# Selective attention and feed-forward on one core: from a planned order to a hand-ordered pipeline of heads and feed-forward pieces

## The chip, the cores and the metric

The kernel runs on one core of one Trainium2 chip. A core has engines that run side by side, each in the order of its own queue: TensorE (PE in the profile; PEld are its weight loads) multiplies matrices and transposes, VectorE (DVE) and ScalarE (ACT) work element by element and read PSUM, where PE writes its results, GpSimd (POOL) works element by element in SBUF, and SyncE (SP) issues the transfers between HBM and SBUF. An engine waits for another through semaphores. The metric is the device time of one execution in microseconds; the time given is the median of several executions.

## What is computed

For 8 batches of 8 heads, with 576 tokens and a head size of 64, causal attention gets a bias from cumulative sums of a positive score `s`. The heads, side by side, are the 512 features of a token. A normalised copy goes through a feed-forward of 2,048 hidden features, and the features themselves are added.

```python
scores = scale * np.matmul(q, k.transpose(0, 1, 3, 2))
s_pos = np.maximum(s, 0.0)
cum = np.cumsum(s_pos, axis=-1)
bias = -(cum[:, :, :, None] - cum[:, :, None, :])
scores = np.where(causal, -1000000000.0, scores + np.minimum(bias, 0.0))
scores = scores - np.max(scores, axis=-1, keepdims=True)
attn = np.exp(scores)
attn = attn / (np.sum(attn, axis=-1, keepdims=True) + 1e-09)
x = np.matmul(attn, v)            # heads laid side by side: (8, 576, 512)
...
xn = (x - mu) / np.sqrt(var + 1e-06) * g_ln
out = x + np.maximum(xn @ w_ch1, 0.0) @ w_ch2
```

Inputs and output are f32; the kernel multiplies in bf16.

## The kernel before

A sequence of 576 tokens is cut in tiles of 128: four full ones and one of 64 (`tsz`). The program is written as one straight sequence, and a scheduler of the framework orders the instructions of each engine from the data dependences and the number of buffers of each pool. So neighbouring heads, and the end of one batch and the start of the next, may be mixed in a queue.

**Preparation.** The first weight is loaded in four pieces of 1 MB, scaled by `g_ln` on VectorE (line 75) and cast on ScalarE (78); the second comes in 16 pieces of 256 KB with casts on ScalarE (84). The cumulative sums of all 64 heads are made at once, in ten doubling steps (94, 95), and put into HBM, once in f32 and once, negated, in bf16.

**Attention**, for each batch: 15 tiles of q, k and v are loaded by SyncE through three buffers and cast on ScalarE (135 to 145). For each head, ten PE transposes (159), each with a copy out of PSUM by VectorE or ScalarE (164), make `qT` and `kT`, 64 rows of 576 columns. A 65th row holds the negated sums in `qT`, brought by a small transfer (152), and ones in `kT`, a memset on GpSimd (151). Five small transfers bring the sums of the keys as a column (172). For each of five key blocks, PE makes the transposed scores for this and all later queries (185), 1,600 columns a head in six matmuls; ScalarE takes the exponential with the keys' sums as bias (194), and GpSimd zeroes what lies above the diagonal (201). Then 15 matmuls of 65 columns multiply by v, whose 65th column of ones gives the denominator (218), and VectorE divides, tile by tile (226, 227).

**Normalisation**, for each batch and tile: statistics on VectorE (238, 240), a square root on ScalarE (242), the normalised row in bf16 (251), four transposes (261) with a copy each (266).

**Feed-forward**, for each batch: 16 blocks of the hidden features, each with four matmuls of 512 columns and four of the 64 left over (277), and a relu of 576 columns on ScalarE (285). Then, for each of five tiles, 16 matmuls of 512 columns (291), the sum with `x_acc` on VectorE (299) and the transfer out (300). The last tile has 64 tokens, and its 16 matmuls still have 512 columns.

## Time and profile before

| what | value |
|---|---|
| median of three executions | 765.15 us (764.25 to 766.16) |
| span of the profiled execution | 764.1 us, 11,760 instructions |
| GpSimd busy | 124.0 us |
| transfers by SP's queue | 46.76 MB in 163,520 packets, 26.6% of 16 engines' span |
| HBM | 37.07 MB read, 9.66 MB written |
| line 277, all forms | 1,000 matmul records, 150.8 us busy |
| line 218, all forms | 960 matmul records, 133.7 us busy |

The profile comes from one further execution, and its span is set beside the median. An engine's busy time is the sum of its instructions' durations; matmuls are pipelined, so that PE may be busy and yet not at its peak, and a matmul's duration holds a delay that the next one overlaps. The pitch, from one start to the next, is then the better measure. The granted clock is the share of TensorE's full clock that it was given.

A row of the grouped instructions reads: line, engine, operation, result <- operands, form, count | busy us, mean ns of one | idle us of the engine just before, and what ended it. A row of stages reads: from:to and length in us, then busy us and count for PE, PEld, DVE, ACT and POOL, then the granted clock, the busy share of the transfer engines and GB/s. A row of the timeline reads: start, length, engine, line, instruction.

### The profile page before, as it was taken

The page shows a single profiled execution, that of the slowest core. Times are in us where ns is not written, and L with a number is a line of the kernel's source. Part 1 is how long each engine was busy: PE and PEld are TensorE (multiplying, and loading weights), DVE is VectorE, ACT ScalarE, POOL GpSimd, SP SyncE. Part 2 cuts the span into 40 slices and gives each one's busy share as a digit, 9 for nine tenths or more (in the row PEclk, how much of TensorE's full clock was granted, in tenths as well). Part 3 has the DMA queues.
Part 4 walks back from the last instruction along what each step waited for, and adds up shares of the span by engine and source line. Part 5 has one row for each costly group of instructions (what it writes and reads, how often), then busy time and mean ns, then how long its engine had stood idle before and what let it go on. Part 6 is the DMA issues. An engine that isn't in the chain of part 4 may idle for free.

```text
span 764.1 us, 11760 instructions
## 1 busy us (share of the span) xinstructions
PE 653.0 (85%) x3772; PEld 323.6 (42%) x3808; DVE 290.2 (38%) x1313; ACT 422.8 (55%) x1006; POOL 124.0 (16%) x390
## 2 busy tenths in 40 slices
PE   0039989997999979998899979999799989999797
PEld 0014434443445434454344434454344544454343
DVE  5215531456015550255314560155503552145601
ACT  4656674667646576256734577065662655255650
POOL 1003300232003310033002320033100330023100
PEclk9999999755895559955697558965599557965599
DMA  9860243522471044101531034200421000100001
GB/s 310 201 134 3 43 111 74 120 43 50 79 185 28 3 84 104 62 2 16 110 91 35 2 57 113 74 9 2 94 60 54 2 2 1 42 23 1 1 1 63
DMA packets 163581, 47.51 MB, mean 62 GB/s; under 512 B 156096, under 2 KB 156224, under 8 KB 163008
## 3 DMA queue, kind: packets, MB, share of 16 engines
q1 hardware_dynamic: 163520, 46.76, 26.6%
q8 instruction: 30, 0.49, 0.3%
q14 instruction: 31, 0.25, 0.1%
HBM read 37.07 MB, written 9.66 MB: 61 GB/s over the span
## 4 chain that ended last, share of the span: by engine, by line
PE 73%; DVE 8%; ACT 7%; DMA 5%; issue 4%; POOL 2%; SPq 1%; DVEq 0%; ACTq 0%
PE ph L277 18%; PE py L291 18%; PE ps L185 13%; PE pt L159 13%; PE pot L218 9%; PE ptx L261 3%; ACT e L194 2%; DVE qT L164 2%; ACT xnT L266 2%; DVE stats L238 2%; DMA qkvtmp<-in_k_dram 2%; POOL kT L151 1%; DMA w2tmp<-in_moe_w_ch_dram 1%; DMA cum_a<-in_s_dram 1%; ACT qT L164 1%
## 5 line engine op out<-in xcount | busy, mean ns | idle before, releaser
L194 ACT ACTIVATE e<-ps,cumk 128x576 bf16<-128x576 f32 (+4 forms) x320 | 158.9, 524 | 70.2 <-PE ps L185 40.8
L201 POOL TENSOR_SCALAR_AFFINE_SELECT e<-e 128x128 bf16<-128x128 bf16 (+1 forms) x320 | 86.8, 280 | 563.0 <-ACT e L194 535.8
L277 PE MATMUL ph<-xnT,w_bf 128*128 128x64 bf16 (+1 forms) x1000 | 150.8, 306 | 1.5 <-ACT hT L285 0.6
L185 PE MATMUL ps<-qT,kT 65*128 65x512 bf16 (+5 forms) x384 | 138.6, 397 | 4.0 <-ACT e L194 3.6
L291 PE MATMUL py<-w_bf,hT 128*128 128x512 bf16 (+1 forms) x628 | 139.4, 379 | 1.0
L218 PE MATMUL pot<-v_bf,e 128*128 128x65 bf16 (+2 forms) x960 | 133.7, 247 | 7.6 <-DVE x_acc L227 3.3
L159 PE MATMUL pt<-ident,q_bf 128*64 128x128 bf16 (+1 forms) x320 | 88.6, 277 | 48.5 <-ACT q_bf L140 30.3
L299 DVE TENSOR_TENSOR yo<-py,x_acc 128x512 f32<-128x512 f32 (+1 forms) x40 | 27.6, 690 | 227.6 <-PE py L291 216.5
L218 PEld LDWEIGHTS <-e 128*128 128x128 bf16 (+2 forms) x960 | 80.2, 127 | 72.4 <-POOL e L201 20.1
L159 PE MATMUL pt<-ident,k_bf 128*64 128x128 bf16 (+1 forms) x320 | 91.1, 285 | 19.6 <-ACT k_bf L145 19.1
L277 PEld LDWEIGHTS <-w_bf 128*128 128x128 bf16 x1024 | 71.0, 103 | 72.8 <-issue 20.2
L285 ACT ACTIVATE hT<-ph 128x576 bf16<-128x576 f32 x128 | 82.9, 649 | 32.3 <-PE ph L277 32.3
L291 PEld LDWEIGHTS <-hT 128*128 128x128 bf16 (+1 forms) x640 | 62.9, 100 | 73.8 <-issue 3.4
L164 DVE COPY qT<-pt 64x128 bf16<-64x128 bf16 (+1 forms) x222 | 46.8, 211 | 112.7 <-PE pt L159 106.2
L227 DVE TENSOR_SCALAR x_acc<-pot,rinv 128x64 f32<-128x64 f32 (+1 forms) x320 | 87.8, 274 | 3.5
L226 DVE RECIPROCAL rinv<-pot 128x1 f32<-128x1 f32 (+1 forms) x320 | 53.1, 166 | 88.3 <-PE pot L218 62.8
L164 ACT COPY qT<-pt 64x128 bf16<-64x128 bf16 (+1 forms) x98 | 22.3, 228 | 93.8 <-PE pt L159 90.7
L159 PEld LDWEIGHTS <-q_bf 128*64 128x64 bf16 (+1 forms) x320 | 41.0, 130 | 65.6 <-ACT q_bf L140 31.1
L159 PEld LDWEIGHTS <-k_bf 128*64 128x64 bf16 (+1 forms) x320 | 41.8, 130 | 63.5 <-issue 34.0
L164 ACT COPY kT<-pt 64x128 bf16<-64x128 bf16 (+1 forms) x132 | 31.5, 239 | 47.9 <-PE pt L159 46.0
L261 PE MATMUL ptx<-ident,xn_bf 128*128 128x128 bf16 (+1 forms) x160 | 36.2, 266 | 25.1 <-DVE xn_bf L251 11.7
L185 PEld LDWEIGHTS <-kT 65*128 65x128 bf16 (+1 forms) x384 | 39.0, 117 | 39.3 <-issue 25.5
(33 smaller groups left out, 323.2 us busy)
## 6 DMA issues: line engine op xcount, KB each, us to landing
qkvtmp<-in_q_dram SPq DMA_DIRECT2D x32, 256.0 KB
qkvtmp<-in_k_dram SPq DMA_DIRECT2D x32, 256.0 KB
qkvtmp<-in_v_dram SPq DMA_DIRECT2D x32, 256.0 KB
out_dram<-yo SPq DMA_DIRECT2D x32, 256.0 KB
w1tmp<-in_moe_w_ch_dram SPq DMA_DIRECT2D x4, 1024.0 KB
w2tmp<-in_moe_w_ch_dram SPq DMA_DIRECT2D x16, 256.0 KB
cumk<-cum_dram SPq DMA_DIRECT2D x256, 0.5 KB
qkvtmp<-in_q_dram SPq DMA_DIRECT2D x8, 128.0 KB
```

The costliest lines, as they stand in the source:

```text
L159: nc.tensor.transpose(pt[:D, :pn], src[:pn, p, h, :], ident[:pn, :pn],)
L164: nc.any.tensor_copy(out=dst[:D, p * P : p * P + pn], in_=pt[:D, :pn])
L185: nc.tensor.matmul(ps[:kbn, o : o + w], lhsT=kT[:D1, kb * P : kb * P + kbn], rhs=qT[:D1, kb * P + o : kb * P + o + w], start=True, stop=True,)
L194: nc.scalar.activation(out=e[:kbn, :qspan], in_=ps[:kbn, :qspan], func=ACT.Exp, bias=cumk[:kbn, kb : kb + 1], scale=1.0,)
L201: nc.gpsimd.affine_select(out=e[:kbn, :kbn], in_=e[:kbn, :kbn], compare_op=ALU.is_ge, fill=0.0, base=0, pattern=[[1, kbn]], channel_multip ...
L218: nc.tensor.matmul(pot[:qn, :], lhsT=e[:kbn, off : off + qn], rhs=v_bf[:kbn, kb, h, :], start=(kb == 0), stop=(kb == t),)
L226: nc.vector.reciprocal(out=rinv[:qn], in_=pot[:qn, D : D + 1])
L227: nc.vector.tensor_scalar_mul(out=x_acc[:qn, t, h * D : (h + 1) * D], in0=pot[:qn, :D], scalar1=rinv[:qn],)
L261: nc.tensor.transpose(pt[:, :qn], xn_bf[:qn, kd * P : (kd + 1) * P], ident[:qn, :qn],)
L277: nc.tensor.matmul(ph[:, o : o + w], lhsT=w1_bf[:, kd, fb * P : (fb + 1) * P], rhs=xnT[:, kd, o : o + w], start=(kd == 0), stop=(kd == KD ...
L285: nc.scalar.activation(out=hT[:, fb, :], in_=ph, func=ACT.Relu)
L291: nc.tensor.matmul(py[:qn, :], lhsT=hT[:, fb, t * P : t * P + qn], rhs=w2_bf[:, fb, :], start=(fb == 0), stop=(fb == FB - 1),)
```

## The change

All of the kernel's body is written anew. The framework's scheduler is switched off (`manual_schedule`): each engine runs its instructions in the order in which the program names them.

- **Slots.** The main loop runs over 64 slots, one head each. A slot names: the weight pieces (batch 0 only), the casts of the tiles loaded in the slot before, two loads for the next batch, in every second slot the transposes of the next two heads, the scores of this head, two feed-forward units, the values of the head before, and two more units.
- **Units.** The feed-forward of a batch is cut in 32 units of four matmuls of 512 columns: 16 for the first layer, with the relu on VectorE in every fourth and on ScalarE otherwise, and 16 quarters of the second. The units of a batch are queued at the end of the second slot of the next one, after its normalisation (`ln_tile`), which is written tile after tile. Its statistics are made in two parts before that, the power -1/2 on GpSimd one slot earlier.
- **Chunks of 512 tokens.** A chunk is a batch's four full tiles. The last 64 tokens of two batches share a tile, `xm`, and the four such tiles are a ninth chunk, run at the end.
- **Bias as contraction rows.** `qT` and `kT` have 68 rows: `qT` holds the negated sums in bf16 and three rows of ones, `kT` ones and the keys' sums in three bf16 parts. A bias on the exponential is no longer needed, so one instruction takes 512 columns of two key blocks at a time. The rows come from SBUF by four transfers for four heads (`aug`). The sums are made by one scan.
- **Transposes for two heads**: a full 128x128 block at a time, five into one PSUM tile, and two copies of 64x640.
- **Casts** of q, k and v stand on ScalarE, VectorE and GpSimd in turn for batch 0, which comes in 30 halves ahead of the slots, and on GpSimd after it. The second weight's casts are on GpSimd too, and the first weight is scaled and cast by one VectorE instruction.

The old lines are those printed above; of the new ones, the core:

```diff
+    stage = ctx.enter_context(tc.tile_pool(name="stage", bufs=8))
+    wst = ctx.enter_context(tc.tile_pool(name="wst", bufs=2))
...
+    xtp = ctx.enter_context(tc.tile_pool(name="xtp", bufs=2))
...
+    ps_s = ctx.enter_context(tc.tile_pool(name="ps_s", bufs=3, space=bass.MemoryType.PSUM))
+    ps_m = ctx.enter_context(tc.tile_pool(name="ps_m", bufs=2, space=bass.MemoryType.PSUM))
+    ps_t = ctx.enter_context(tc.tile_pool(name="ps_t", bufs=2, space=bass.MemoryType.PSUM))
+    ps_o = ctx.enter_context(tc.tile_pool(name="ps_o", bufs=1, space=bass.MemoryType.PSUM))
+    ctx.enter_context(tc.manual_schedule())
...
+    qT = [const.tile([P, G, SP], BF16, name=f"qT{i}") for i in range(2)]
+    kT = [const.tile([P, G, SP], BF16, name=f"kT{i}") for i in range(2)]
+    e2 = [const.tile([P, 2, EW], BF16, name=f"e2_{i}") for i in range(3)]
+    xm = [const.tile([P, Dm], F32, name=f"xm{i}") for i in range(4)]
+    xTm = const.tile([P, KD, 512], BF16, name="xTm")
...
+    def load(src, b, t, h0, h1, eng):
+        pn = P if t < NF else TL
+        tmp = stage.tile([P, h1 - h0, D], F32, name="qkvtmp", tag="st")
+        eng.dma_start(
+            out=tmp[:pn],
+            in_=src[b, h0:h1, t * P : t * P + pn, :].rearrange("h s d -> s h d"),
+        )
+        return tmp, pn
+    def cast(kind, b, t, h0, h1, tmp, pn, eng):
+        if kind == "v":
+            dst = v_bf[b % 2][:pn, t, h0:h1, 0:D]
+        else:
+            dst = (q_bf if kind == "q" else k_bf)[b % 2][:pn, t, h0:h1, :]
...
+    for i in range(2):
+        nc.gpsimd.memset(q_bf[i][TL:P, NF, :, :], 0.0)
+        nc.gpsimd.memset(k_bf[i][TL:P, NF, :, :], 0.0)
+        nc.vector.memset(v_bf[i][:, 0:NF, :, D : D + 1], 1.0)
+        nc.vector.memset(v_bf[i][TL:P, NF, :, :], 0.0)
+        nc.vector.memset(v_bf[i][0:TL, NF, :, D : D + 1], 1.0)
+        nc.gpsimd.memset(qT[i][D:KA, :, :], 1.0)
+        nc.gpsimd.memset(kT[i][D:KA, :, :], 1.0)
+    for i in range(3):
+        nc.gpsimd.memset(e2[i][TL:P, :, OD : OD + TL], 0.0)
+        nc.gpsimd.memset(e2[i][:, :, OD + TL : EW], 0.0)
+    nc.vector.tensor_tensor_scan(
+        out=c_sc, data0=c_one, data1=c_in, initial=0.0, op0=ALU.mult, op1=ALU.add
+    )
...
+    def aug(b, g):
+        r0 = b * H + g * G
+        i = (b * 2 + g) % 2
+        for j, src in ((1, c_hi), (2, c_mid), (3, c_lo)):
+            nc.sync.dma_start(out=kT[i][D + j : D + j + 1, :, 0:S], in_=src[r0 : r0 + G, :])
+        nc.sync.dma_start(out=qT[i][D : D + 1, :, 0:S], in_=c_neg[r0 : r0 + G, :])
+    def qk_pair(b, j):
+        g, i = j // 2, (b * 2 + j // 2) % 2
+        hh = (j % 2) * 2
+        for src, dst in ((k_bf, kT), (q_bf, qT)):
+            tr = ps_t.tile([P, SP], BF16, name="trqk", tag="tr")
+            for t in range(NT):
+                nc.tensor.transpose(
+                    tr[:, t * P : (t + 1) * P],
+                    src[b % 2][:, t, 2 * j : 2 * j + 2, :],
+                    ident,
+                )
+            nc.vector.tensor_copy(out=dst[i][0:D, hh, :], in_=tr[0:D, :])
+            nc.vector.tensor_copy(out=dst[i][0:D, hh + 1, :], in_=tr[D : 2 * D, :])
...
+    def scores(b, h):
+        i, hh = (b * 2 + h // G) % 2, h % G
+        kk, qq = kT[i], qT[i]
+        e, u = e_of(b, h)
+        def mm(dst, kb, q0, q1):
+            nc.tensor.matmul(
+                dst,
+                lhsT=kk[0:KA, hh, kb * P : (kb + 1) * P],
+                rhs=qq[0:KA, hh, q0:q1],
+                start=True,
+                stop=True,
+            )
+        a = ps_s.tile([P, 512], F32, name="sa", tag="s")
+        mm(a, 0, 0, 512)
+        nc.scalar.activation(out=e[:, u, 0:512], in_=a, func=ACT.Exp)
+        a = ps_s.tile([P, 512], F32, name="sb", tag="s")
+        mm(a[:, 0:64], 0, 512, 576)
+        mm(a[:, 64:512], 1, 128, 576)
+        nc.scalar.activation(out=e[:, u, OB : OB + 512], in_=a, func=ACT.Exp)
+        a = ps_s.tile([P, 512], F32, name="sc", tag="s")
+        mm(a[:, 0:320], 2, 256, 576)
+        mm(a[:, 320:512], 3, 384, 576)
+        nc.scalar.activation(out=e[:, u, OC : OC + 512], in_=a, func=ACT.Exp)
+        for o in (0, OB + 64, OC, OC + 320):
+            nc.gpsimd.affine_select(
+                out=e[:, u, o : o + P],
+                in_=e[:, u, o : o + P],
+                compare_op=ALU.is_ge,
+                fill=0.0,
+                base=0,
+                pattern=[[1, P]],
+                channel_multiplier=-1,
+            )
+    def scores_d(b, j):
+        i = (b * 2 + j // 2) % 2
+        e, _ = e_of(b, 2 * j)
+        d = ps_t.tile([P, 2, TL], F32, name="sd", tag="tr")
+        for u in range(2):
+            hh = (2 * j + u) % G
+            nc.tensor.matmul(
+                d[:, u, :],
+                lhsT=kT[i][0:KA, hh, NF * P : SP],
+                rhs=qT[i][0:KA, hh, NF * P : S],
+                start=True,
+                stop=True,
+            )
+        nc.scalar.activation(out=e[0:TL, :, OD : OD + TL], in_=d[0:TL], func=ACT.Exp)
+        nc.gpsimd.affine_select(
+            out=e[0:TL, :, OD : OD + TL],
+            in_=e[0:TL, :, OD : OD + TL],
+            compare_op=ALU.is_ge,
+            fill=0.0,
+            base=0,
+            pattern=[[0, 2], [1, TL]],
+            channel_multiplier=-1,
+        )
...
+        pot = ps_o.tile([P, NT, D + 1], F32, name="pot", tag="pot")
+        for t in range(NT):
+            last = min(t, NF)
+            for kb in range(last + 1):
+                o = KOFF[kb] + t * P if t < NF else TAIL[b % 2][kb]
+                nc.tensor.matmul(
+                    pot[:, t, :],
+                    lhsT=e[:, u, o : o + P],
+                    rhs=vv[:, kb, h, :],
+                    start=(kb == 0),
+                    stop=(kb == last),
+                )
+        rinv = small.tile([P, NT], F32, name="rinv", tag="rinv")
+        nc.vector.reciprocal(out=rinv, in_=pot[:, :, D])
+        hs = slice(h * D, (h + 1) * D)
+        nc.vector.tensor_tensor(
+            out=xb[b][:, :, hs],
+            in0=pot[:, 0:NF, 0:D],
+            in1=rinv[:, 0:NF].unsqueeze(2).to_broadcast([P, NF, D]),
+            op=ALU.mult,
+        )
+        ps = slice(0, TL) if b % 2 == 0 else slice(TL, P)
+        nc.vector.tensor_scalar_mul(
+            out=xm[b // 2][ps, hs], in0=pot[ps, NF, 0:D], scalar1=rinv[ps, NF : NF + 1]
+        )
...
+    def ln_aggr(b):
+        n = len(x_tiles(b))
+        mv = small.tile([P, 5, 2], F32, name="mv", tag="mv", bufs=2)
+        rs = small.tile([P, 5], F32, name="rs", tag="rs", bufs=2)
+        for t in range(n):
+            nc.vector.bn_aggr(out=mv[:, t, :], in_=st[b][:, t, :, :])
+        nc.vector.tensor_scalar_add(out=rs[:, 0:n], in0=mv[:, 0:n, 1], scalar1=1e-6)
+        nc.gpsimd.tensor_tensor(
+            out=rs[:, 0:n], in0=rs[:, 0:n], in1=mhalf[:, 0:n], op=ALU.pow
+        )
+        mvs[b] = (mv, rs)
+    xTs = {}
+    def ln_tile(b, t):
+        x = x_tiles(b)[t]
+        mv, rs = mvs[b]
+        if t == 0:
+            xTs[b] = xtp.tile([P, KD, 512], BF16, name="xT", tag="xT")
+        xn = xnp.tile([P, Dm], BF16, name="xn", tag="xn")
+        nc.vector.tensor_scalar(
+            out=xn,
+            in0=x,
+            scalar1=mv[:, t, 0:1],
+            scalar2=rs[:, t : t + 1],
+            op0=ALU.subtract,
+            op1=ALU.mult,
+        )
+        tr = ps_t.tile([P, KD, P], BF16, name="trx", tag="tr")
+        for kd in range(KD):
+            nc.tensor.transpose(tr[:, kd, :], xn[:, kd * P : (kd + 1) * P], ident)
+        if t < NF:
+            dst = xTs[b][:, :, t * P : (t + 1) * P]
+        else:
+            dst = xTm[:, :, (b // 2) * P : (b // 2 + 1) * P]
+        nc.vector.tensor_copy(out=dst, in_=tr)
+    def mlp1(xT, fb, on_dve):
+        ph = ps_m.tile([P, 512], F32, name="ph", tag="m")
+        for kd in range(KD):
+            nc.tensor.matmul(
+                ph,
+                lhsT=w1_bf[:, kd, fb * P : (fb + 1) * P],
+                rhs=xT[:, kd, :],
+                start=(kd == 0),
+                stop=(kd == KD - 1),
+            )
+        if on_dve:
+            nc.vector.tensor_scalar_max(out=hT[:, fb, :], in0=ph, scalar1=0.0)
+        else:
+            nc.scalar.activation(out=hT[:, fb, :], in_=ph, func=ACT.Relu)
...
+    def mlp2(t, quarter, x, dst):
+        if quarter == 0:
+            py[0] = ps_m.tile([P, Dm], F32, name="py", tag="m")
+        for fb in range(quarter * 4, quarter * 4 + 4):
+            nc.tensor.matmul(
+                py[0],
+                lhsT=hT[:, fb, t * P : (t + 1) * P],
+                rhs=w2_bf[:, fb, :],
+                start=(fb == 0),
+                stop=(fb == FB - 1),
+            )
+        if quarter == 3:
+            yo = yop.tile([P, Dm], F32, name="yo", tag="yo")
+            nc.vector.tensor_add(out=yo, in0=py[0], in1=x)
+            dst(yo)
+    def chunk_units(xT_of, x_of, dst_of):
+        for fb in range(FB):
+            yield lambda fb=fb: mlp1(xT_of(), fb, fb % 4 == 3)
+        for t in range(NF):
+            for qr in range(4):
+                yield lambda t=t, qr=qr: mlp2(t, qr, x_of(t), dst_of(t))
...
+    engs = ("act", "dve", "pool")
+    done = 0
+    def more(n, t, h0, h1):
+        first_tmp.append(load(SRC[n], 0, t, h0, h1, nc.sync))
+    first += [("v", t, 0, 4) for t in range(NT)]
+    order0 = first + [(n, t, 4, 8) for t in range(NT) for n in ("k", "q")]
+    order0 += [("v", t, 4, 8) for t in range(NT)]
+    for i, (n, t, h0, h1) in enumerate(order0):
+        if i + 6 < len(order0):
+            more(*order0[i + 6])
+        if i == 2:
+            aug(0, 0)
+        if i == 8:
+            aug(0, 1)
+        tmp, pn = first_tmp[i]
+        cast(n, 0, t, h0, h1, tmp, pn, engs[i % 3])
+        if i == 9:
+            qk_pair(0, 0)
...
+    def w1_part(c, kd):
+        tmp = wst.tile([P, 1024], F32, name="w1tmp", tag="w")
+        sl = slice(c * 1024, (c + 1) * 1024)
+        nc.sync.dma_start(out=tmp, in_=w1_r[:, kd, sl])
+        nc.vector.tensor_scalar_mul(
+            out=w1_bf[:, kd, sl], in0=tmp, scalar1=gln[:, kd : kd + 1]
+        )
+    def w2_part(c):
+        tmp = wst.tile([P, 2, Dm], F32, name="w2tmp", tag="w")
+        nc.sync.dma_start(out=tmp, in_=w2_r[:, 2 * c : 2 * c + 2, :])
+        nc.gpsimd.tensor_copy(out=w2_bf[:, 2 * c : 2 * c + 2, :], in_=tmp)
...
+    def run_units(n):
+        for _ in range(n):
+            if queue:
+                queue.pop(0)()
+    slots = [(b, h) for b in range(B) for h in range(H)]
+    loads = {}
+    for n_, (b, h) in enumerate(slots):
+        if b == 0:
+            for i in (2 * h, 2 * h + 1):
+                if i < 8:
+                    w1_part(i // 4, i % 4)
+                else:
+                    w2_part(i - 8)
+        for n, lb, t, tmp, pn in loads.pop(n_, []):
+            cast(n, lb, t, 0, H, tmp, pn, "pool")
+        if b + 1 < B:
+            items = [(n, t) for t in range(NT) for n in ("k", "q")] + [("v", t) for t in range(NT)]
+            for n, t in items[2 * h : 2 * h + 2]:
+                tmp, pn = load(SRC[n], b + 1, t, 0, H, nc.sync)
+                loads.setdefault(n_ + 1, []).append((n, b + 1, t, tmp, pn))
+        if h % 2 == 0:
+            nb, nj = (b, h // 2 + 1) if h < 6 else (b + 1, 0)
+            if nb < B:
+                qk_pair(nb, nj)
+        scores(b, h)
+        if h % 2 == 0:
+            scores_d(b, h // 2)
+        run_units(2)
+        if pend:
+            pb, ph_ = pend.pop(0)
+            pv(pb, ph_)
+            if ph_ == 3:
+                if pb + 1 < B:
+                    aug(pb + 1, 0)
+            if ph_ == 7 and pb + 1 < B:
+                aug(pb + 1, 1)
+            if ph_ == 5:
+                ln_stats(pb, 0)
+            if ph_ == 7:
+                ln_stats(pb, 1)
+                ln_aggr(pb)
+        pend.append((b, h))
+        run_units(2)
+        if h == 1 and b > 0:
+            for t in range(len(x_tiles(b - 1))):
+                ln_tile(b - 1, t)
+            queue += batch_units(b - 1)
+    pv(*pend.pop(0))
+    ln_stats(B - 1, 1)
+    ln_aggr(B - 1)
+    run_units(6)
+    for t in range(NT):
+        ln_tile(B - 1, t)
+    run_units(len(queue))
+    queue += batch_units(B - 1)
+    queue += mixed_units()
+    run_units(len(queue))
```

344 lines of the change are left out of this document (109 added, 235 removed).

## The prediction

> **What bounds the kernel now.** The page comes first: busy times, the granted clock in forty slices, and the chain that ended last.
>
> ```profile
> span 764.1 us, 11760 instructions
> PE 653.0 (85%) x3772; PEld 323.6 (42%) x3808; DVE 290.2 (38%) x1313; ACT 422.8 (55%) x1006; POOL 124.0 (16%) x390
> PEclk9999999755895559955697558965599557965599
> PE 73%; DVE 8%; ACT 7%; DMA 5%; issue 4%; POOL 2%; SPq 1%; DVEq 0%; ACTq 0%
> ```
>
> PE carries the end, and its clock swings. The busy times by stage (count of matmuls first, clock near the end of a row) say when:
>
> ```profile
> 56.00:92.00 36.00, 35.10 (x203) 17.42 (x202) 20.67 (x110) 21.30 (x54) 13.35 (x42) 1.00 0.17 24
> 146.00:182.00 36.00, 34.27 (x208) 17.81 (x206) 20.55 (x112) 23.77 (x60) 13.39 (x42) 0.50 0.23 41
> 94.00:106.20 12.20, 8.03 (x39) 3.50 (x39) 8.18 (x34) 8.57 (x27) 1.12 (x4) 1.00 0.40 89
> 106.20:140.20 34.00, 33.55 (x205) 16.42 (x208) 3.54 (x7) 16.95 (x32) 0.00 (x0) 1.00 0.49 114
> 285.95:289.36 3.41, 3.41 (x17) 1.48 (x16) 0.00 (x0) 1.16 (x2) 0.00 (x0) 0.50 0.38 83
> 292.77:296.18 3.41, 3.41 (x28) 1.74 (x27) 0.00 (x0) 3.23 (x6) 0.00 (x0) 1.00 0.52 118
> 139.17:142.58 3.41, 2.69 (x16) 1.31 (x15) 0.95 (x3) 2.44 (x10) 0.00 (x0) 1.00 0.84 186
> 235.00:323.60 88.60, 81.16 (x467) 40.20 (x470) 33.87 (x158) 49.18 (x122) 15.11 (x47) 0.69 0.25 55
> 126.55 13.23 PE py L291 x60
> ```
>
> A batch takes 88.6 us (last windows row): attention some 43, normalisation some 12, feed-forward 34. In the feed-forward PE runs without a gap: 60 matmuls of 512 columns in 13.23 us are 0.22 us each at clock 1.00, and first-layer matmuls pass 28 per 3.41 us at 1.00 against 17 at 0.50. Attention runs at 0.50. The first row's 1.00 is only the absence of a record: batch 0 passes as many matmuls in 36 us as batch 1 at 0.50. So half the kernel is attention and normalisation with PE waiting on hand-overs or at half clock. The clock rises in the first dense stretch and falls in the first stretch of 3.41 us that the feed-forward ends in. In attention a head streams 1,152 transpose columns, 1,600 score columns and 975 value columns; at 0.22/512 x 2 us per column that is 3.2 us of the 36/206 x 31 = 5.4 that a head of 31 matmuls takes, 59%: too little to raise the clock.
>
> **The change, part by part.** Small operations, from the timeline at half clock:
>
> ```profile
> 66.22 0.31 PE L159 MATMUL pt<-ident,q_bf 128*64 128x128 bf16 x1
> 66.33 0.31 PE L159 MATMUL pt<-ident,k_bf 128*64 128x128 bf16 x1
> 68.08 0.24 PE L218 MATMUL pot<-v_bf,e 128*128 128x65 bf16 x1
> 68.54 0.35 PE L218 MATMUL pot<-v_bf,e 128*128 128x65 bf16 x3
> ```
>
> A transpose starts 0.11 us after the one before it; three value matmuls end 0.11 after one would, so 0.055 each. At full clock these lie between half and all of that: I take 0.07 and 0.04, the middle.
>
> PE per head slot, with feed-forward pieces: 4 units of 4 matmuls, 16 x 0.22 = 3.5; scores 1,600 x 0.22/512 = 0.7; values 15 x 0.04 = 0.6; transposes, now for two heads at once, 5 x 0.07 = 0.35; hand-overs not shown, 0 to 0.8, I take 0.3. Sum **5.45 us**. Streaming share (8,192 + 1,600 + 975 + 640 columns) x 0.00043 = 4.9 of 5.45, 90%: near the feed-forward's, so I forecast full clock inside the slots.
>
> The other engines need rows by form:
>
> ```profile
> L194 ACT ACTIVATE e<-ps,cumk 128x576 bf16<-128x576 f32 x64 | 47.4, 740 | 18.2 <-PE ps L185 14.3 <-issue 3.1 <-POOL kT L151 0.3
> L194 ACT ACTIVATE e<-ps,cumk 128x448 bf16<-128x448 f32 x64 | 40.1, 627 | 1.5 <-PE ps L185 1.5
> L285 ACT ACTIVATE hT<-ph 128x576 bf16<-128x576 f32 x128 | 82.9, 649 | 32.3 <-PE ph L277 32.3
> L164 DVE COPY qT<-pt 64x128 bf16<-64x128 bf16 x207 | 44.1, 213 | 110.7 <-PE pt L159 104.9 <-DMA cumk<-cum_dram 0.4
> L164 DVE COPY qT<-pt 64x64 bf16<-64x64 bf16 x15 | 2.7, 179 | 2.0 <-PE pt L159 1.3
> L226 DVE RECIPROCAL rinv<-pot 128x1 f32<-128x1 f32 x256 | 43.0, 168 | 61.2 <-PE pot L218 53.3
> L227 DVE TENSOR_SCALAR x_acc<-pot,rinv 128x64 f32<-128x64 f32 x256 | 70.6, 276 | 2.7
> L299 DVE TENSOR_TENSOR yo<-py,x_acc 128x512 f32<-128x512 f32 x32 | 22.1, 692 | 204.5 <-PE py L291 193.5 <-remote 11.0
> L238 DVE BATCH_NORM_STATS2 stats<-x_acc 128x6 f32<-128x512 f32 x32 | 21.2, 662 | 0.0
> L251 DVE TENSOR_SCALAR xn_bf<-x_acc,mv,rstd 128x512 bf16<-128x512 f32 x32 | 16.4, 532 | 0.0
> L266 DVE COPY xnT<-ptx 128x128 bf16<-128x128 bf16 x22 | 4.7, 217 | 7.0 <-PE ptx L261 6.9
> L201 POOL TENSOR_SCALAR_AFFINE_SELECT e<-e 128x128 bf16<-128x128 bf16 x256 | 74.8, 292 | 562.2 <-ACT e L194 535.0 <-PE pot L218 10.4 <-DVE rinv L226 7.9
> L201 POOL TENSOR_SCALAR_AFFINE_SELECT e<-e 64x64 bf16<-64x64 bf16 x64 | 14.9, 232 | 0.8 <-ACT e L194 0.8
> L151 POOL MEMSET kT<- 1x576 bf16 x64 | 36.5, 571 | 28.2 <-POOL e L201 27.3
> ```
>
> ACT: the first two rows give 0.88 ns a column, so an exponential of 512 takes 0.68; three and half a small one (0.36), 2.2 us; up to three relus of 0.59: at most 4.0. The relus queue behind the exponentials, and the third unit waits for the first one's buffer: 2.2 + 0.59 after the first score, when PE has done scores, two units and values (3.0). It is free just in time. Casts and square roots have left ACT.
>
> DVE: copies of 64x640 at 0.52 ns a column, 0.48 x 2 a slot; reciprocal 0.17; the scaling of 256 columns 0.42 and of the last tile 0.28; a relu or final sum of 0.69; statistics and normalised rows, 4.5 tiles a batch x (0.8 + 0.17 + 0.53 + 0.4) / 8 = 1.1. Sum 3.6 us, under PE's 5.45. In slots that begin with transposes the copies queue behind the previous slot's 0.69, and the small scores wait 0.4 for their buffer; that is in my 0.3 hand-over.
>
> Pool: the two masks give 0.94 ns a column, so a cast of 512 columns, which no row shows, 0.65; 15/8 a slot and 1.3 of masks: 2.5. The cast is bounded below by nothing and above by several us (rival).
>
> At nothing I cost: the bias as contraction rows (68 rows where 65 stood, same columns); the four small transfers that bring them, queued on SP four slots ahead of their scores; the some 380 small transfers that go, since SP's queue has 1% of the chain; the power on Pool for the standard deviation, one slot ahead of its use, which would show only from some 5 us.
>
> So **54 slots x 5.45 = 294 us**: of 64, batch 0 and two of batch 1 have no pieces.
>
> **Normalisation** is written tile by tile: DVE makes a tile, PE transposes it, DVE copies it, and only then makes the next. PE and DVE hold their own order, so nothing covers it: 0.53 + four transposes (0.55 with the result's delay) + 0.4 + two hand-overs = 1.65 us a tile. The first also waits behind the last slot's final sum. PE loses 7.0 us for four tiles, 8.65 for five, 6.3 in batch 0: 6.3 + 3 x 7.0 + 3 x 8.65 = **53 us**. This gap is longer than the 3.41 us stretch that lost the clock above, so the clock falls; it comes back after one full dense stretch, some 5 us later, half lost: 7 x 2.3 = **16 us**.
>
> [...]
>
> **Start.** Transfers and the resources that start them:
>
> ```profile
> GB/s 310 201 134 3 43 111 74 120 43 50 79 185 28 3 84 104 62 2 16 110 91 35 2 57 113 74 9 2 94 60 54 2 2 1 42 23 1 1 1 63
> L135 SPq DMA_DIRECT2D qkvtmp<-in_q_dram x40: 368/532/1498, 4.2 to 559.0; - x40
> 36.36 4.54 DMA qkvtmp<-in_k_dram
> L75 DVE TENSOR_SCALAR w1tmp<-w1tmp,gln_sb 128x2048 f32<-128x2048 f32 x4 | 5.1, 1280 | 6.3 <-DMA w1tmp<-in_moe_w_ch_dram 6.3
> 760.29 0.68 DVE L299 TENSOR_TENSOR yo<-py,x_acc 64x512 f32<-64x512 f32 x1 [2.88 <-PE py L291]
> ```
>
> Pool first fills four rows of 2,560 columns (0.99 ns each, memset row), tails and masks: 14 us. Its first cast frees stage buffer 2, for which SP's eleventh load waits; SP then has 20 loads and 4 bias rows of 0.5 each: 15 + 12 = 27, landing and cast 2 more. ACT's casts stand ahead of its first exponential: slots begin at **29 us**.
>
> In batch 0 each slot brings 1 MB of weights and 0.5 of the next batch, with two weight buffers; DVE's scaling (0.64 for 1,024 columns), then Pool's casts, wait for them in order, ahead of the copies and masks that PE needs. At 310 GB/s 1.5 MB take 4.8 us; I take 5.5 for the round trip (4.8 to 7): **44 us**. Two slots of batch 1 without pieces at half clock: **7**.
>
> **End.** Values 0.6, six units 5.3, five tiles 8.7, two units 1.8, then 64 units without heads, 256 x 0.22 = 56.3; clock 2.3; after the last matmul the trace of before needs 764.1 - 760.3 = 3.8. Sum **79**.
>
> Nine chunks of 128 matmuls are 253 us where 8 x 34 = 272 stood; the rest of the gain is attention covered by the pieces. Total span: 29 + 44 + 7 + 53 + 294 + 16 + 79 = **522**. The median before is 765.15, 1.05 above the span: **523 us**.
>
> **Rivals.**
> 1. The clock does not hold in the slots. At half clock a slot costs 7.0 + 1.4 + 0.8 + 0.55 + 0.3 = 10.05. For: every attention stretch at 0.50. Against: 90% streaming. Half the slots: 523 + 27 x 4.6 = 647; all of them, without the 16: 755. Chance 0.14, at 647.
> 2. The overlap fails in the queues: the two unit buffers wait each time for a relu (0.65 and 0.2 of hand-over, twice a slot). For: ACT is just in time above. 523 + 54 x 1.7 = 615. Chance 0.11.
> 3. Pool and DVE exclude each other in SBUF: Pool's 2.5 and DVE's 3.6 make a slot of 6.1, 523 + 54 x 0.65 = 558. No row shows it; Pool's casts are new. [...] Chance 0.12.
> 4. **Slower.** Pool becomes the bound: masks queue behind casts, values behind masks. It decides from a cast of (5.45 - 1.3) x 8/15 = 2.2 us; the 46 slots that load need 242/46 = 5.3 us more each to reach 765, a cast of 5 us: 800 with one of 5.4. Against: masks at 0.94 ns a column, eight times less. Chance 0.03.
>
> The forecast keeps 0.60. Its own bounds: slot 4.9 to 6.1, batch 0 38 to 56, start 22 to 33, normalisation 40 to 60, clock 8 to 30: some 485 to 565. Range, with rivals 2 and 3 and short of 1 and 4: 485 to 620.
>
> A difference of 0.3% is about what a measurement here can tell. Faster by more: all cases but rival 4 and the far end of rival 1 (755 and a little over), 0.96; within: 0.01, that end; slower: 0.03.
>
> **What would show it.** Clock 1.00 in most stretches of batches 2 to 6; heads every 5.45 us; a gap of 7 to 8.7 us in PE's matmuls once a batch with DVE, PE and DVE in turn; Pool's cast near 0.65; the first exponential near 29 us and batch 1 near 73; the last 64 units in 56 us. A clock of 0.50 between normalisations, a relu as releaser of units, or a cast over 2.2 us would make it wrong.

## The result, and the profile after

The changed kernel takes **503.25 us** (502.84 to 504.88) where the kernel before takes 765.64 in the same comparison: a ratio of 0.657, with a 95% interval of 0.656 to 0.659. The forecast was 523, in a range of 485 to 620. The profiled execution has a span of 503.2 us. First the lines of its page that answer to those shown of before: span, busy times, clock by slices, and the chain that ended last.

```profile
span 503.2 us, 8135 instructions
PE 397.9 (79%) x2960; PEld 212.6 (42%) x2960; DVE 245.9 (49%) x614; ACT 174.1 (35%) x343; POOL 174.9 (35%) x439
PEclk9998555699959995999599979997999799999999
PE 69%; DVE 14%; DMA 8%; POOL 5%; issue 1%; SPq 1%; POOLq 0%
```

PE is still the chain, with 2,960 matmul records where the kernel before has 3,772, and its clock is at full rate from the third slot of batch 1 on (some 98 us), but for one dent in each batch. Nearly all the rest is told by six stages of the changed kernel, in the view of busy times by stage: the first from the first exponential to batch 1's first score, the next two to the end of batch 0's normalisation and then to the end of the last slot, two plain slots, a stretch with a normalisation and the slot that it ends, and the last two chunks.

```profile
31.40:77.00 45.60, 20.85 (x188) 14.26 (x189) 21.31 (x51) 13.52 (x29) 23.45 (x52) 0.66 0.96 261
77.00:92.60 15.60, 8.39 (x71) 5.65 (x69) 9.14 (x29) 3.29 (x7) 10.16 (x23) 0.50 0.88 160
92.60:427.50 334.90, 297.19 (x2360) 160.45 (x2358) 179.73 (x465) 137.57 (x273) 122.71 (x335) 0.92 0.36 78
161.80:172.20 10.40, 9.94 (x85) 5.39 (x84) 5.53 (x14) 4.98 (x10) 4.74 (x13) 1.00 0.01 2
130.80:144.90 14.10, 8.60 (x68) 5.04 (x66) 8.54 (x26) 1.58 (x3) 4.54 (x9) 0.77 0.81 169
442.40:498.60 56.20, 56.20 (x256) 24.68 (x254) 11.07 (x16) 14.33 (x24) 0.00 (x0) 1.00 0.13 38
```

Two plain slots take 10.4 us, and PE is busy in 9.94 of them, with the clock at 1.00; no other engine passes 5.6. The timeline of PE over these two slots shows every piece of the forecast's sum:

```profile
161.82 0.38 PE L189 MATMUL sa<-qT,kT 68*128 68x512 bf16 x1
162.04 0.38 PE L189 MATMUL sb<-qT,kT 68*128 68x64 bf16 x2
162.25 0.38 PE L189 MATMUL sc<-qT,kT 68*128 68x320 bf16 x2
162.47 1.89 PE L339 MATMUL ph<-xT,w_bf 128*128 128x512 bf16 x8
164.20 0.61 PE L260 MATMUL pot<-v_bf,e 128*128 128x65 bf16 x15
164.65 1.89 PE L339 MATMUL ph<-xT,w_bf 128*128 128x512 bf16 x8
166.38 0.44 PE L172 MATMUL trqk<-ident,k_bf 128*128 128x128 bf16 x5
166.66 0.44 PE L172 MATMUL trqk<-ident,q_bf 128*128 128x128 bf16 x5
166.94 0.38 PE L189 MATMUL sa<-qT,kT 68*128 68x512 bf16 x1
...
167.37 0.38 PE L189 MATMUL sc<-qT,kT 68*128 68x320 bf16 x2
168.22 0.23 PE L225 MATMUL sd<-qT,kT 68*128 68x64 bf16 x2 [0.47 <-DVE kT L178]
168.29 1.89 PE L357 MATMUL py<-w_bf,hT 128*128 128x512 bf16 x8
```

Read it by the starts. Scores take 0.65 us (161.82 to 162.47), eight unit matmuls 1.73, fifteen value matmuls 0.45, five transposes 0.28, and each follows the last without a gap. The only wait is at the small scores (`sd`), for VectorE's copies of the transposed heads: 0.47 us of idle time, and 0.63 by the starts, since the scores ahead of it, begun at 166.94, would have made room at 167.59.

The normalisation, by contrast, is the bare chain that was forecast. The timeline, VectorE and PE by turns:

```profile
135.61 0.69 DVE L366 TENSOR_TENSOR yo<-py,xb 128x512 f32<-128x512 f32 x1 [0.89 <-PE py L357]
136.22 0.54 DVE L319 TENSOR_SCALAR xn<-xb,mv,rs 128x512 bf16<-128x512 f32 x1
136.82 0.40 PE L329 MATMUL trx<-ident,xn 128*128 128x128 bf16 x4 [1.24 <-DVE xn L319]
137.25 0.42 DVE L334 COPY xT<-trx 128x512 bf16<-128x512 bf16 x1 [0.49 <-PE trx L329]
137.59 0.90 DVE L319 TENSOR_SCALAR xn<-xb,mv,rs 128x512 bf16<-128x512 f32 x1
138.55 0.61 PE L329 MATMUL trx<-ident,xn 128*128 128x128 bf16 x4 [1.33 <-DVE xn L319]
139.19 0.43 DVE L334 COPY xT<-trx 128x512 bf16<-128x512 bf16 x1 [0.70 <-PE trx L329]
```

Final sum, row, transposes, copy, next row: 1.73 us from the first transposes to the second, and PE does nothing but four transposes in it. The next three pitches are 1.58 us; the one shown is longer because its row took 0.90 where the others took 0.54.

### The profile page after: what moved, and what is told of

It reads as the page before. It is cut to its first block, busy times and chain, and to the rows that moved or that the text cites. A ratio compares the mean times of both kernels' runs of the same rounds, so it can differ in the third digit from the quotient of the medians.

```text
span 503.2 us, 8135 instructions
## 1 busy us (share of the span) xinstructions
PE 397.9 (79%) x2960; PEld 212.6 (42%) x2960; DVE 245.9 (49%) x614; ACT 174.1 (35%) x343; POOL 174.9 (35%) x439
## 4 chain that ended last, share of the span: by engine, by line
PE 69%; DVE 14%; DMA 8%; POOL 5%; issue 1%; SPq 1%; POOLq 0%
PE ph L339 27%; PE py L357 25%; PE pot L260 5%; DMA w1tmp<-in_moe_w_ch_dram 4%; PE trx L329 4%; DVE xn L319 3%; DMA w2tmp<-in_moe_w_ch_dram 3%; DVE xT L334 2%; DVE kT L178 2%; PE sb L189 2%; PE sc L189 2%; PE sa L189 2%; DVE yo L366 2%; DVE hT L347 2%; PE trqk L172 2%; DVE kT L177 2%
## 5 line engine op out<-in xcount | busy, mean ns | idle before, releaser
L357 PE MATMUL py<-w_bf,hT 128*128 128x512 bf16 x576 | 135.2, 383 | 0.0
L209 POOL TENSOR_SCALAR_AFFINE_SELECT e<-e 128x128 bf16<-128x128 bf16 x256 | 71.7, 295 | 169.1 <-ACT e L199 150.6
L339 PE MATMUL ph<-xT,w_bf 128*128 128x512 bf16 x512 | 129.3, 400 | 0.0
L199 ACT ACTIVATE e<-sa 128x512 bf16<-128x512 f32 x64 | 38.2, 597 | 189.8 <-PE sa L189 183.2
L349 ACT ACTIVATE hT<-ph 128x512 bf16<-128x512 f32 x108 | 64.8, 600 | 80.4 <-PE ph L339 79.8
L339 PEld LDWEIGHTS <-w_bf 128*128 128x128 bf16 x576 | 55.2, 101 | 62.4 <-issue 13.3
L357 PEld LDWEIGHTS <-hT 128*128 128x128 bf16 x576 | 53.6, 98 | 56.8 <-issue 1.6
L260 PEld LDWEIGHTS <-e 128*128 128x128 bf16 x960 | 41.5, 103 | 23.4 <-POOL e L209 8.3
L260 PE MATMUL pot<-v_bf,e 128*128 128x65 bf16 x960 | 44.5, 202 | 7.0 <-POOL e L209 7.0
L189 PEld LDWEIGHTS <-kT 68*128 68x128 bf16 x320 | 28.8, 109 | 25.1 <-issue 8.5
L207 ACT ACTIVATE e<-sc 128x512 bf16<-128x512 f32 x64 | 38.7, 605 | 0.0
L203 ACT ACTIVATE e<-sb 128x512 bf16<-128x512 f32 x64 | 37.9, 592 | 0.0
L366 DVE TENSOR_TENSOR yo<-py,xb 128x512 f32<-128x512 f32 x32 | 22.1, 690 | 25.8 <-PE py L357 25.3
L172 PE MATMUL trqk<-ident,k_bf 128*128 128x128 bf16 x160 | 18.5, 256 | 18.9 <-POOL k_bf L123 14.1
```

The source lines that it names most:

```text
L189: nc.tensor.matmul(dst, lhsT=kk[0:KA, hh, kb * P : (kb + 1) * P], rhs=qq[0:KA, hh, q0:q1], start=True, stop=True,)
L199: nc.scalar.activation(out=e[:, u, 0:512], in_=a, func=ACT.Exp)
L203: nc.scalar.activation(out=e[:, u, OB : OB + 512], in_=a, func=ACT.Exp)
L207: nc.scalar.activation(out=e[:, u, OC : OC + 512], in_=a, func=ACT.Exp)
L209: nc.gpsimd.affine_select(out=e[:, u, o : o + P], in_=e[:, u, o : o + P], compare_op=ALU.is_ge, fill=0.0, base=0, pattern=[[1, P]], channe ...
L260: nc.tensor.matmul(pot[:, t, :], lhsT=e[:, u, o : o + P], rhs=vv[:, kb, h, :], start=(kb == 0), stop=(kb == last),)
```

## The experiments

Times are medians; each set was run beside the kernel before, whose medians were 765.6 to 767.0, so that a difference of some 0.2% between sets says nothing. The changed kernel's 503.25 (0.656 to 0.659 of before) is what they are held against.

### Pieces in one block

```diff
             queue += batch_units(b - 1)
+            run_units(len(queue))
```

> The 32 feed-forward units of a batch run in one block after its normalisation instead of two by two between the heads; every instruction and the rest of the order stay. Theory (the gain is cover and clock: pieces fill PE while a head's exponentials and copies run, and hold the clock at 1.00): heads without pieces fall back to 0.50 and some 3.4 us a slot, the block takes 32 x 0.87 = 27.8 us and 2.5 to warm up, normalisation 7.7: 65 us a batch where 51.7 stand, 7 times: 570 to 620 us, clock near 0.50 in all slots. Rival (fewer and larger instructions and the casts off ScalarE make the gain, the interleaving adds little): 520 us or less.

Measured: **581.9 us**, ratio 0.760 (0.757 to 0.762): the theory's range, with a result that corrects the forecast's own emphasis. Six slots of batch 2, then the 32 units of a block, by stage:

```profile
185.50:203.10 17.60, 14.64 (x160) 9.61 (x158) 12.59 (x36) 9.88 (x21) 11.33 (x33) 0.71 0.92 184
155.90:185.20 29.30, 29.18 (x129) 12.99 (x131) 5.12 (x9) 7.17 (x12) 0.00 (x0) 0.95 0.07 28
```

Heads on their own take 2.9 us each (17.6 / 6) where the kernel before took 5.4. This is a mean over two clocks: the first three, still at 1.00 behind the block, take 2.4 each (185.54 to 192.82), the next three, at 0.50, 3.4 (192.82 to 203.13), as expected. At 1.00 the columns of such a head are 1.4 of its 2.4 us, by the forecast's price, and the clock does not hold. At the forecast's price of a column at half clock a head's 3,215 columns are now 2.8 of these 3.4 us, where 3.2 of 5.4 stood. So of the 262 us that the change gains, 184 (765.6 to 581.9) are there without any cover, and the interleaving is worth the other 79. The 184 lie in the heads for the most part: a batch takes some 62 us here for 88.6, of which the block makes up 29.3 for 34 and these six heads 17.6 for 32. Which of their new parts does it was not taken apart.

### Normalised rows ahead

```diff
-    xnp = ctx.enter_context(tc.tile_pool(name="xnp", bufs=3))
-    xtp = ctx.enter_context(tc.tile_pool(name="xtp", bufs=2))
+    xnp = ctx.enter_context(tc.tile_pool(name="xnp", bufs=5))
+    xtp = ctx.enter_context(tc.tile_pool(name="xtp", bufs=1))
...
+        if h == 1 and b > 0:
+            for t in range(len(x_tiles(b - 1))):
+                ln_norm(b - 1, t)
         scores(b, h)
```

`ln_norm` holds the row's instruction, `ln_tile` what is left.

> VectorE makes all normalised rows of a batch ahead of the second slot's scores, and only transposes and copies stay at its end (five row buffers for three, one transposed buffer for two). Theory (the gap once a batch is the chain VectorE, PE, VectorE of 1.6 us a tile): the gap in PE falls from 7.0 (four tiles) and 8.4 (five) to 3 to 4 us, 7 batches: 465 to 480 us, and the clock may or may not fall. Rival (VectorE as a whole is the limit there, so that the rows made earlier only push the division and the final sum back by as much): 498 to 505.

Measured: **463.9 us**, ratio 0.606 (0.602 to 0.609), a little better than the theory's range. The stretch that was shown above with 14.1 us, by stage here, and this kernel's clock by slices:

```profile
129.40:138.60 9.20, 6.95 (x67) 4.27 (x66) 8.23 (x25) 1.57 (x3) 5.54 (x9) 1.00 0.51 131
```

```profile
PEclk9999999999999999999999999999999999999999
```

4.9 us less for five tiles, and in this execution the clock never falls after it has risen. What is left of the gap is one wait for VectorE, whose first copy now stands behind the rows, the division and the final sum:

```profile
136.53 0.71 PE L335 MATMUL trx<-ident,xn 128*128 128x128 bf16 x8 [1.94 <-DVE xT L340]
```

VectorE is busy for 8.2 of the 9.2 us.

### Filling the gap with matmuls

```diff
+    def fill(n):
+        pf = ps_m.tile([P, 512], F32, name="pf", tag="m")
+        for _ in range(n):
+            nc.tensor.matmul(pf, lhsT=ident, rhs=w2_bf[:, 0, :], start=True, stop=True)
...
             for t in range(len(x_tiles(b - 1))):
+                fill(6 if t == 0 else 4)
                 ln_tile(b - 1, t)
```

> Matmuls of 512 columns whose result nobody reads stand ahead of each tile's transposes in the normalisation: six before the first, four before each other. They fit in the time that PE waits there. Theory (the fall of the clock is a cost of its own): the clock stays at 1.00 from the first unit on, the slot after each normalisation loses its 0.4 to 1.9 us, and the transposes run at full clock: 488 to 495 us. Rival (the gap alone costs, the clock little): 500 to 506; a time above 506 means that the filling itself lengthens the chain.

Measured: **484.9 us**, ratio 0.633 (0.631 to 0.635): 18.4 us less, by adding 160 matmuls (154 in the records) that do nothing, and more than was expected. The stretch with the normalisation, and the slot after it:

```profile
128.60:141.60 13.00, 11.99 (x89) 5.92 (x89) 8.39 (x26) 1.57 (x3) 4.71 (x9) 1.00 0.86 179
141.60:146.20 4.60, 4.55 (x41) 2.41 (x40) 2.29 (x7) 3.36 (x7) 2.52 (x7) 1.00 0.11 13
```

At clock 1.00 the stretch is 1.1 us shorter and the slot after it takes 4.6 us; in the changed kernel that slot, at a mean clock of 0.70, takes 6.5:

```profile
144.90:151.40 6.50, 6.50 (x40) 3.07 (x39) 2.32 (x7) 3.51 (x7) 2.51 (x7) 0.70 0.00 0
```

The expectation had measured the loss against a plain slot of 5.2. But the slot after a normalisation has no wait at its small scores, since no relu or final sum stands ahead of the copies on VectorE, and is 4.6 us long at full clock. Added up over the profiled executions, the seven slots behind a normalisation lose 13.9 us (46.4 to 32.5) and the six stretches of batches 1 to 6 lose 4.5 (77.3 to 72.9): 18.4, the whole gain.

### Twice GpSimd's casts

```diff
             cast(n, lb, t, 0, H, tmp, pn, "pool")
+            cast(n, lb, t, 0, H, tmp, pn, "pool")
```

> Each cast of q, k and v on GpSimd in the slots is done twice, into the same place: 1.2 us more of GpSimd in 46 slots. Theory (PE is the bound of a slot, GpSimd has some 2.7 us of slack): 501 to 508 us. Rival 3 of the prediction (GpSimd and VectorE exclude each other in SBUF, and their sum is near the slot): up to 46 x 1.2 = 55 us more, 520 to 558.

Measured: **508.2 us**, ratio 0.664 (0.662 to 0.665), a little above the theory's range (501 to 508). The two plain slots, by stage:

```profile
162.80:173.20 10.40, 9.88 (x85) 5.41 (x85) 5.56 (x14) 4.98 (x10) 7.27 (x18) 1.00 0.00 0
```

GpSimd has 7.27 us where it had 4.74, and the slots are as long as before to the hundredth; VectorE's busy time is the same (5.56 us for 5.53), and the two engines' busy times, 12.8 us, no longer fit in the slots one behind the other. The profiled execution is 3.1 us longer, and this comes elsewhere: batch 1 begins 2.3 us later, behind the slots of batch 0 in which GpSimd also casts weights, and its first two slots take 0.9 more. Rivals 3 and 4 are out for the slots.

### Small scores behind the first units

```diff
-        if h % 2 == 0:
-            scores_d(b, h // 2)
         run_units(2)
+        if h % 2 == 0:
+            scores_d(b, h // 2)
```

> The two small score matmuls of every second slot stand behind the slot's first two units instead of ahead of them. Theory (PE is the bound of a slot, and the 0.47 us that it waits there for VectorE's copies of the transposed heads is time lost): 27 such slots with units x 0.47 = 12.7 us less, 489 to 493 us, slots of 4.6 and 4.8 us in place of 5.12 and 5.27 by turns summing to 10.4. Rival (VectorE's queue or the two unit buffers set the slot, the wait moves to the next unit): 500 to 504.

Measured: **489.1 us**, ratio 0.638 (0.636 to 0.641). Two slots now, by stage:

```profile
153.80:163.50 9.70, 9.65 (x86) 5.42 (x84) 4.80 (x13) 6.67 (x13) 4.80 (x13) 1.00 0.49 105
```

PE is busy for 9.65 of 9.70 us, and by the starts of the scores two slots take 5.12 + 4.63 = 9.75. This is the sum of PE's work, 2 x (3.46 + 0.65 + 0.45) + 0.56 + 0.07 = 9.75, where the last two are the ten transposes and the two small scores; the wait did not move on. That the gain, 14.2 us, is so near the 12.7 expected is partly luck: 27 slots at 0.47 were counted, while in the changed kernel's trace 19 slots have the wait (5.27 us long where the others have 5.12), and each of them loses 0.64 (5.27 to 4.63).

### The scheduler left on

```diff
-    ctx.enter_context(tc.manual_schedule())
```

> The same program with the framework's scheduler left on: it may reorder each engine's queue by what it believes ready, and the order written by hand is only its priority. Theory (most of the gain is that the pieces stand between the heads, which the program's order gives the scheduler too; the normalisation's chain could even be covered): 450 to 520 us. Rival (the queues' exact order is what keeps PE full): above 540.

Measured: **451.6 us**, ratio 0.588 (0.587 to 0.590). The order written by hand costs 51.6 us against the same program in the scheduler's order. Two rows on ScalarE, of the changed kernel and of this one, show a first gain, and PE's timeline of this one inside a normalisation a second; how the 51.6 us divide between them was not measured:

```profile
31.39 0.58 ACT L199 ACTIVATE e<-sa 128x512 bf16<-128x512 f32 x1
```

```profile
19.07 0.60 ACT L198 ACTIVATE e<-sa 128x512 bf16<-128x512 f32 x1 [1.62 <-PE sa L188]
```

```profile
128.68 0.39 PE L328 MATMUL trx<-ident,xn 128*128 128x128 bf16 x2 [3.94 <-DVE xn L318]
128.86 0.63 PE L188 MATMUL sa<-qT,kT 68*128 68x512 bf16 x1
129.29 0.42 PE L328 MATMUL trx<-ident,xn 128*128 128x128 bf16 x2
129.50 0.63 PE L188 MATMUL sb<-qT,kT 68*128 68x64 bf16 x2
```

The first exponential no longer stands behind the casts of the whole batch, and scores of the next heads stand between the transposes of the rows, though a wait of 3.94 us stays ahead of the first.

### Fills behind the loads

```diff
+    def late_fills():
+        fills(1)
+        for i in range(3):
+            nc.gpsimd.memset(e2[i][TL:P, :, OD : OD + TL], 0.0)
+            nc.gpsimd.memset(e2[i][:, :, OD + TL : EW], 0.0)
+    fills(0)
...
-        if i == 8:
-            aug(0, 1)
...
+    late_fills()
+    aug(0, 1)
     nc.sync.dma_start(out=gln, in_=moe_g_ln.rearrange("(kd p) -> p kd", p=P))
```

`fills(i)` is the old fill of group i.

> GpSimd fills only what the first group of heads needs ahead of its first casts; the second group's rows, tails and mask areas, and the second group's four bias transfers, come behind the 30 halves of batch 0. Theory (the start is set by GpSimd's 14 us of filling, by the bias rows for which SP waits, and by the loads queued behind them): the first exponential comes 5 to 9 us earlier than at 31.4, 494 to 499 us; the casts of the bias parts on VectorE, 1.07, 2.25 and 1.67 us beside GpSimd's filling, shrink to about 0.6. Rival (the transfers of batch 0 set the start): 502 to 505.

Measured: **507.7 us**, ratio 0.662 (0.660 to 0.663): slower by 4.5, though the first exponential came 5.5 us earlier, as the theory has it. Of this kernel:

```profile
8.68 0.45 DVE L159 CAST c_mid<-c_in 64x576 bf16<-64x576 f32 x1
...
25.84 0.58 ACT L204 ACTIVATE e<-sa 128x512 bf16<-128x512 f32 x1
...
32.15 0.65 SPq L167 DMA_DIRECT2D kT<-c_hi  x1
...
35.24 0.98 SPq L425 DMA_DIRECT2D w1tmp<-in_moe_w_ch_dram  x2
```

and of the changed kernel:

```profile
8.40 2.22 POOL L141 MEMSET qT<- 4x2560 bf16 x1
8.68 2.25 DVE L154 CAST c_mid<-c_in 64x576 bf16<-64x576 f32 x1
10.58 2.53 POOL L142 MEMSET kT<- 4x2560 bf16 x1
...
30.62 0.97 SPq L420 DMA_DIRECT2D w1tmp<-in_moe_w_ch_dram  x2
```

SP waits until 32.15 us for the late fills before it sends the second group's bias rows, and the first weight piece, queued behind them, goes out at 35.24 and not at 30.62. The heads' 5.5 us are no gain where the weights set the pace of batch 0, and the weights came 4.6 us later.

### All of it, and where the rows stand

The next kernel has the rows ahead, their transposes spread between the second slot's units and copied by ScalarE, the small scores behind the units, and the late fills.

```diff
+                if t in (2, 4):
+                    run_units(1)
                 ln_tile(b - 1, t)
...
-        nc.vector.tensor_copy(out=dst, in_=tr)
+        nc.scalar.copy(out=dst, in_=tr)
```

> All of it together: normalised rows ahead, their transposes spread between the second slot's units with the copies on ScalarE, the small scores behind the first units, the fills behind the loads. If the gains are separate parts of PE's one chain they add up: 464 (rows ahead alone) less 12.7, less 5 to 9, less 10 to 16 for what is left of the gap: 425 to 438 us, the clock at 1.00 from the first unit on. If they share a limit (VectorE or GpSimd in the slots): 445 to 455.

Measured: **442.1 us**, ratio 0.576 (0.575 to 0.577): between the two. The sum had counted the late fills as a gain of 5 to 9 where they lose 4.5. So the bias rows were moved, to the second slot and then to the fourth:

```diff
-    aug(0, 1)
...
+        if n_ == 1:
+            aug(0, 1)
```

> All of it, with one thing moved: the second group's four bias transfers come in the second slot, behind the first weight pieces, and no longer ahead of them, where SP waited until 32 us for GpSimd's late fills. Theory (batch 0 is bound by its transfers, whose engines are 0.96 busy there, and so by the moment at which the weights start): the weights start near 25 us where they started at 35, batch 1's first score near 73 where it stood at 82, 431 to 435 us. Rival (batch 0 is bound by the round trips and hand-overs in its slots): 437 to 443.

> As the run with the rows in the second slot, but the four transfers stand in the fourth slot, where GpSimd's late fills are long done, so that SP waits for them nowhere. Theory (what counts is when the weights move): the second pair of weight pieces, issued at 35.0 us there, goes out near 30, batch 1's first score comes near 71 to 73 in place of 75.2, 431 to 434 us. Rival: 436, as there.

Measured: **436.5 us** (ratio 0.570, 0.568 to 0.572), above its theory's range, then **434.1** (0.566, 0.564 to 0.569), at the edge of its own. The two intervals overlap, so the step from one to the other is not shown. The weights start at 25.1 us in both, and batch 1's first score comes at 75.25 and 74.66, where 73 and 71 to 73 were expected. In the first SP waited for the fills again, ahead of the second pair; in the second that pair went at 33.0, when a weight buffer came free, and not near 30:

```profile
30.16 2.22 POOL L142 MEMSET kT<- 4x2560 bf16 x1
30.20 3.43 DVE L431 TENSOR_SCALAR w_bf<-w1tmp,gln 128x1024 bf16<-128x1024 f32 x2 [3.00 <-DMA w1tmp<-in_moe_w_ch_dram]
32.96 1.03 SPq L430 DMA_DIRECT2D w1tmp<-in_moe_w_ch_dram  x2
```

The late fills still hold the weights back, by another way. VectorE's scaling of the first piece, 0.75 us in the changed kernel, takes some 2.7 beside GpSimd's fill (3.43 for the two), and its buffer comes free some 2 us later. Batch 0 shows 0.91 of the transfer engines' time used. Last, a third weight buffer, with one output buffer fewer:

```diff
-    wst = ctx.enter_context(tc.tile_pool(name="wst", bufs=2))
+    wst = ctx.enter_context(tc.tile_pool(name="wst", bufs=3))
```

> The kernel of the run beside it with three weight buffers for two (and two output buffers for three). Theory (in batch 0 the 16 transfer engines are the bound, 0.96 busy in the changed kernel): 0 to 3 us less. Rival (the round trip through two buffers is the bound, as a 5.5 us slot was worked out): 5 us less or more.

Measured: **431.0 us**, ratio 0.562 (0.561 to 0.564), the fastest kernel of the study: 3.1 us less, at the upper end of the theory. Batch 0 by stage, with two buffers and then with three:

```profile
25.90:74.70 48.80, 20.98 (x189) 14.32 (x190) 24.07 (x54) 13.35 (x28) 31.04 (x62) 1.00 0.91 245
```

```profile
25.90:70.90 45.00, 20.11 (x188) 13.86 (x189) 24.18 (x54) 13.84 (x29) 31.30 (x62) 0.72 0.98 267
```

3.8 us shorter, and the transfer engines at 0.98, so that a further buffer has little left to gain there.

### The mended order against the scheduler

The kernel with the rows in the second slot, with `manual_schedule` taken out.

> The kernel of the run beside it with the framework's scheduler left on. Theory (with the normalisation covered, the hand order has PE full in the slots, and the scheduler can only win in batch 0, where it lets heads run ahead of late weights): 425 to 440 us, within 2% of it. Rival (the scheduler's gain over the hand order, 51.6 us in the unmended kernel, comes from more than the normalisation): below 420.

Measured: **443.6 us**, ratio 0.579 (0.578 to 0.581), 7 us behind the same kernel's hand order (436.5), and within 2% of it, if a little above the theory's range. With the normalisation covered, the small scores moved and the start mended, the hand order wins; which of these turned the balance was not taken apart.

## Why the prediction was right, step by step

The measured parts of the profiled execution add up as the forecast's did: 31.4 + 45.6 + 15.6 + 334.9 + 75.7 = 503.2. Four of the five lie within 3.3 us of the forecast, and their errors largely cancel (2.4 + 1.6 + 2.3 - 3.3 = 3.0).

- **Start**: forecast 29, measured 31.4 to the first exponential. The mechanism is the one named, GpSimd's fills and SP's queue: the run with late fills moved it to 25.8. A part of it was not seen: VectorE's casts of the bias parts wait for GpSimd's fills (1.07, 2.25 and 1.67 us).
- **Batch 0**: forecast 44, measured 45.6, with 0.96 of the transfer engines' time used, which leaves little for the round trip through two buffers that the forecast added. In the mended kernel, where the share was 0.91, a third buffer took 3.1 us off.
- **Two slots and batch 0's normalisation**: forecast 13.3 (7 + 6.3), measured 15.6.
- **Slots, normalisation and clock of batches 1 to 6**: forecast 294 + 47 + 16 = 357, measured 334.9. This is the whole error. Some 14 us of it lie in the slot, sized at 5.45 us and 5.19 long. Values were taken at 0.04 us each and take 0.030, transposes at 0.07 and take 0.056, scores at 0.7 and take 0.65; the hand-over of 0.3 was right, since the 0.63 at every second slot's small scores come to 0.32 a slot, by the mechanism that the forecast gave. The middle between half and all of a price at half clock was the wrong choice: at full clock the price is near half (0.030 of 0.055, 0.056 of 0.11). Another 6 us lie in the clock: the seven slots behind a normalisation take 5.65 to 7.15 us, 6.6 in the mean, where 5.45 + 2.3 were forecast.
- **Normalisation**: forecast 8.65 us for five tiles and 7.0 for four. The second slot less a plain one is 8.9, 8.3 and 8.5 us with five, and 7.0, 7.0 and 6.5 with four. Moving the rows took 39.3 us off the kernel (503.25 to 463.9), clock included, so the gap was where it was said to be.
- **Clock**: forecast 16 and 2.3. The filled gaps gain 18.4 us: against a slot of 5.19 the fall costs only some 10, but at full clock these slots need no more than 4.6, which the forecast had not seen. No run shows a cost of 30 us, the most that its bounds allow for the clock: the runs showed 18.4. Rival 1 is out: a clock of 1.00 in the plain slots of batches 2 to 7.
- **End**: forecast 79, measured 75.7; the 64 last units 56.2 for 56.3.
- **Rivals 2, 3 and 4** are out. No relu holds a unit up: PE has no idle time ahead of its unit matmuls (0.0 us in the changed kernel). That GpSimd and VectorE exclude each other was an assumption, and the slots do not show it: VectorE is busy for 5.56 us of two slots beside twice the casts and for 5.53 without, though waiting of this kind does occur elsewhere (below). A cast takes 0.61 us for the 0.65 taken.

What was wrong, though it moved no number, is the sentence that the rest of the gain is attention covered by pieces. With the pieces apart 70% of the gain remains. Which of the other parts makes it (transposes for two heads, exponentials over two key blocks, copies and casts moved, chunks of 512 tokens) was not taken apart: it stays open. And the forecast took the new order of the queues as given; what it costs by itself, 51.6 us, was seen only with the scheduler on. The forecast did price one part of it, the uncovered normalisation.

## What to carry to other kernels

A hand-made order is as good as its worst stage: look for the place where two engines hand one tile back and forth in the order of the program, and write the first engine's part for all tiles ahead. Price a stage that will run at full clock from half of what the trace shows at half clock, and not from the middle: here 0.055 became 0.030 and 0.11 became 0.056. Before moving work off a queue's head, ask what stands behind its new place: the late fills gained 5.5 us for the first exponential and cost the weights 4.6.

## What the runs showed of the hardware that was not expected

- **Idle matmuls pay.** In the changed kernel's normalisation PE runs four transposes in 1.6 us and the clock falls to 0.50 every time, seven times in all; with four more matmuls of 512 columns beside them it holds at 1.00, and 18.4 us are won. With the rows made ahead the clock held too, at 1.00 in the profiled execution, with a wait of 1.94 us in PE where the stretch is 4.0 us longer than a plain slot.
- **VectorE's casts wait for GpSimd's fills.** The cast of 64x576 f32 to bf16 takes 2.25 us while GpSimd fills, in the changed kernel, and 0.45 while it doesn't, in the run with late fills. In the changed kernel three casts of this size, begun during a fill, take 1.07, 2.25 and 1.67 us, and each ends 0.31 or 0.32 us after the fill does. A normalised row beside a GpSimd cast took 0.90 where its neighbours took 0.54. For the casts of 64x576 that makes five times the length at worst. In the plain slots it cost nothing that the run with twice the casts could show (10.4 us for two slots in both), since VectorE is not the bound there; in the mended kernels it held a weight buffer some 2 us longer.
